# Loads from a second queue, another split of the weights' decoding over the engines, and a packed composition in the opening of a light-convolution and maxout kernel

## The chip, the core and the metric

The kernel runs on one core of one Trainium2 chip. TensorE (PE in the profile) multiplies, VectorE (DVE), ScalarE (ACT) and GpSimd (POOL) do the work on elements, and SyncE (SP) and, if the program asks for it, other engines issue transfers to and from the memory of the chip (DRAM). Work tiles lie in SBUF; the products of TensorE land in PSUM, in eight banks. The metric is the device time of one execution in microseconds (us), the median of several.

## The reference

Two steps follow one another. `x` is 8 x 4160 x 192 and `weight_gen` 8 x 4160 x 8 x 7.

```python
w = softmax(weight_gen, over the 7 taps)          # per position and head
x_unf[b, s, k] = x_pad[b, s + k]                  # 6 zero rows ahead of each batch row
out = einsum('bshk,bskhg->bshg', w, x_unf)        # 8 heads of 24 channels
x = out.reshape(33280, 192)
h = maximum(maximum(x @ w1, x @ w2), x @ w3)      # each 192 x 768
return (h @ w_out).astype(float32)                # 768 x 192
```

The four weight matrices arrive as 64-bit floats, two 32-bit words for each number. The kernel reads the words and makes 32-bit floats of them itself.

## The kernel before

Tokens are worked in 65 chunks of 512. For each chunk the seven taps are softmaxed (ACT, DVE, POOL), x is multiplied by them (`r`, seven shifted products of 192 channels, 128 x 1344 elements, mostly on POOL, for a few tiles on DVE), summed over the taps (`acc`, on DVE), and turned so that channels lie along the partitions. In the opening, the tiles of chunk 0 and 1 are turned by TensorE against the identity; tiles listed in `ADDED_AS_TURNED` skip the sum on DVE, since TensorE turns all seven products and adds them in PSUM. Of the turned chunk and of each weight a high and a low part are made (`xa_hi`, `xa_lo`, `wa_hi`, `wa_lo`; channels 128 to 191 are `xb`, `xc`, `wb_hi`, `wb_lo`), and TensorE multiplies the parts that count. The three products of an up step are reduced to their maximum by differences: TensorE forms x (w1 - w3) and the like, and DVE and ACT take maxima and add. From chunk 2 on the same program runs for each chunk (line L1287 is nearly all of it).

The opening differs. The list `OPENING` is walked by a planner (`Plan`), which places each step's instructions on the engines' queues by costs, due times and a list of shifts (`moved`). The order within each queue is then fixed; an engine waits for an instruction's inputs with everything behind it.

- Loads: `load_a` (L772, the first 128 rows of w1, w2, w3 for a pair of 128-column blocks, 128 x 512 words), `load_b` (L788, the last 64 rows, for one or two pairs, on both partition halves), `load_down` (L806, w_out, 128 x 768 words). All are issued by SP. What is loaded borrows room of other tiles, so the profile calls it `h_hi`, `raw`, `room` or `h_lo`.
- Decoding: `single` turns word pairs into 32-bit floats. ACT takes the magnitude of the high word (L832). The clamp to the 32-bit range is by POOL or DVE (L849) or by two scalings on ACT (L842). Then DVE makes three passes: shift and mask (L856), the sign out of the high word (L865), the top bits of the low word (L874). The running value `ui()` of all three lies in PSUM (`bank`). A decoded piece is called `wx` (w2 and w3), `w1a` (w1), `b` (last rows), `wo` (w_out).
- Differences: POOL subtracts w1 (`h_lo<-wx,w1a`, L1017; `b<-b`, L942). For chunk 0 these 32-bit differences are multiplied directly (`up_whole`, L1349 and L1356). ACT makes the high parts (L1042, L1089, and four half copies L1108 per pair), POOL or DVE the low ones (L1004).
- TensorE in the opening: products against the identity (`warm`, L898), turns of x (L576 for the added tiles, L613 and L614 for the others), turns of w1 (L1156, L1157), three pairs of up products, the composition w1 w_out (L1181: six products of 64 output rows for channels 128 to 191, then six of 128), the down products of chunk 0 (L1436, L1438, L1445), then chunk 1's up products, the first rows of L1287.

Of the kernel before, what the change touches and what calls it, by code (L numbers as in the profile page):

```python
# [12 lines left out]
U32 = mybir.dt.uint32  # L13
AF = mybir.ActivationFunctionType
# [185 lines left out]
def lightconv_maxout_kernel(  # L200
# [31 lines left out]
    ADDED_AS_TURNED = ((0, 1), (0, 2), (0, 3))  # L232
# [3 lines left out]
    ON_POOL_FIRST = (0, 1, 2, 3)  # L236
    TAPS_ON_VECTOR = ((0, 0), (2, 3), (3, 2))
# [7 lines left out]
    CLAMP_ON_POOL = (('a', 0, 0), ('a', 1, 0), ('a', 2, 0), ('b', 0))  # L245
    CLAMP_ON_SCALAR = (('a', 0, 1), ('a', 1, 1), ('d', 0), ('d', 1), ('d', 2))
# [5 lines left out]
         ('d',): -86.4,  # L252
         ('s', 0): -96.4,
         ('s', 1): -99.4}
# [16 lines left out]
    for c in range(supers[-1][-1] + 1, NC):  # L271
        if len(supers) == len(SUPERS) or len(supers[-1]) == SC or place[c] != place[c - 1] + 1:
# [4 lines left out]
    F_MAX = float(np.array(0x47EFFFFF, np.uint32).view(np.float32))  # L277
    F_MIN = float(np.array(0x38000000, np.uint32).view(np.float32))
# [6 lines left out]
         ('warm', 1), ('warm', 1), ('warm', 1), ('warm', 2), ('warm', 18), ('turn x', 0, 3),  # L285
         ('turn x', 0, 2), ('warm', 3), ('turn x', 0, 0), ('turn x', 0, 1), ('warm', 2),
         ('warm', 1), ('warm', 4), ('warm', 1), ('turn', 0), ('warm', 4), ('parts', 0),
         ('a', 0, 0, 1), ('a', 0, 1, 2), ('b', 0), ('up', 0, 0), ('a', 1, 0, 2), ('b', 1),
         ('up', 0, 2), ('turn', 1), ('turn', 2), ('a', 2, 0, 2), ('b', 2), ('up', 0, 4),
         ('compose', 1), ('compose', 0), ('turn x', 1, 2), ('turn x', 1, 0), ('turn x', 1, 1),  # L290
         ('turn x', 1, 3), ('down', 0), ('parts', 1), ('up', 1, 2), ('up', 1, 1), ('up', 1, 0),
         ('up', 1, 3), ('up', 1, 4), ('up', 1, 5))
# [6 lines left out]
    wb_hi = const.tile([P, NJ, NI, P], F32R, name="wb_hi")  # L299
# [28 lines left out]
        "bhi": ([P, NI, P], F32R),  # L328
# [5 lines left out]
        "bhi": 2, "raw": 1,  # L334
# [9 lines left out]
        for name, n in counts.items()  # L344
    }
    plan = Plan(counts | {"conv": 3, "flight": 8}, ((3, -26.38), (4, 3.87), (5, -21.88), (7, -1.3), (9, -9.51), (11, -9.72), (12, -18.74),
# [12 lines left out]

    def hold(name):  # L360
        return Hold(name)
# [14 lines left out]
    def act(n):  # L376
        return 0.08 + 0.00083 * n
# [17 lines left out]
    def transfer(cost, emit, deps=(), due=None, holds=(), on="SP", issue=0.46):  # L395
        held = [*holds, hold("flight")]
        begun = plan.add(on, issue, emit, deps, due, held)
        return plan.add("DMA", cost, lambda: None, [begun], due, held, end=cost + 2.4)
# [367 lines left out]

    def load_a(jp):
        for i, w in enumerate(words[:3]):
            a_in[jp, i] = transfer(
                0.67,  # L770
                lambda i=i, w=w: pin(
                    nc.sync.dma_start(  # L772
                        out=raw_a(jp)[:, i].rearrange("p n w -> p (n w)"),
                        in_=w[:P, 4 * jp * P : 4 * (jp + 1) * P],
                    )
                ),
                (), LOAD_DUE["a", jp] + 0.1 * i, [a_hold(jp)],
            )

    def load_b(first, last):  # L780
        got = []
        for i, w in enumerate(words[:3]):
            for odd, h in enumerate(halves):
                got.append(
                    transfer(
                        0.05 + 0.29 * (last - first),
                        lambda i=i, w=w, odd=odd, h=h: pin(
                            nc.sync.dma_start(  # L788
                                out=raw_b()[h, first:last, i].rearrange("p j n w -> p j (n w)"),
                                in_=w[P:].rearrange("p (j o n) -> p j o n", j=NP, o=2)[  # L790
                                    :, first:last, odd
                                ],
                            )
                        ),
                        (), LOAD_DUE["b", first], [hraw[2]], issue=0.62,
                    )
                )
        for jp in range(first, last):
            b_in[jp] = got
# [14 lines left out]
    def single(key, n, source, target, deps, holds):  # L814
# [5 lines left out]
        def like(v):  # L820
            s = source().shape
            return v if len(s) == 3 else v.rearrange("p (i n) -> p i n", n=s[2])

        u = lambda: like(buf(hu)[:, :n])
# [8 lines left out]
                    u(), high().bitcast(F32), AF.Abs, scale=2.0**111 if by_scalar else 1.0  # L833
# [4 lines left out]
        if by_scalar:  # L838
            for scale in (2.0**-111, 2.0**-112):
                a = plan.add(  # L840
                    "ACT", act(n),
                    lambda scale=scale: pin(nc.scalar.activation(u(), u(), AF.Copy, scale=scale)),  # L842
                    [a], None, [hu],
                )
            b, keep, sign = a, 0x7FFFFFF8, 0x80000000
        else:
# [5 lines left out]
            keep, sign = 0x3FFFFFF8, 0xC0000000  # L852
        c = plan.add(
# [218 lines left out]
    def differences_b(jp):  # L1072
        hq = hold("bhi")
        on, then = MODE["b", jp]
        v, d, holds, terms = difference(
            (NI, P), lambda: b32[:, jp, 1:], lambda: b32[:, jp, 0], [one_b[jp]], [], on
        )
        if jp in WHOLE_UP:
            then = "POOL" if then == "L" else then
            if on == "L":  # L1080
                of = v
                d = plan.add(
                    "ACT", act(2 * P), lambda: pin(nc.scalar.copy(b32[:, jp, 1:], of())), [d],
                    None, holds,
                )
                v, holds = (lambda: b32[:, jp, 1:]), []
        b_32[jp] = d
        e = plan.add(
            "ACT", act(2 * P), lambda: pin(nc.scalar.copy(buf(hq), v())), [d], None, [*holds, hq]  # L1089
        )  # L1090

        def low():
            b_lo[jp] = rest(
                2 * P, lambda: wb_lo[:, jp], v, lambda: buf(hq).bitcast(F32), [e],
                [hq] if then == "L" else [*holds, hq], then, terms,
                2.2 if jp in WHOLE_UP or on == "POOL" else 1.0,
            )

        if then == "L":
            later["b", jp] = [low]  # L1100
        else:
            low()
        for odd, h in enumerate(halves):
            b_hi[2 * jp + odd] = [
                plan.add(
                    "ACT", 0.42,
                    lambda to=to, h=h, odd=odd: pin(
                        nc.scalar.copy(wb_hi[to, 2 * jp + odd], buf(hq)[h].bitcast(F32))  # L1108
                    ),
                    [e], None, [hq],  # L1110
                )
                for to in halves
            ]
# [58 lines left out]

    def compose(n):
        for to, f in (((wca, slice(0, P)), (wcb, slice(P, D)))[n],):
# [136 lines left out]
    def up(c, j, i):  # L1311
# [5 lines left out]
        def terms(half):  # L1317
            got = [
# [3 lines left out]
                    (CH, lambda: wb_hi[:, j, i], lambda: buf(b), [*b_hi[j], bl], [b])  # L1322
                    if half == low
                    else (CH, lambda: wb_hi[:, j, i], lambda: buf(k), [*b_hi[j], *cs], [k])
# [52 lines left out]
    def evict(c, j, i, hb, made):  # L1377
# [7 lines left out]
        hh, hl, his, los = hs[c]  # L1385
        if i == 0:
# [39 lines left out]
    def down_whole(t):  # L1426
        assert len(of_c32) == 3
# [47 lines left out]
    def down(c, t):  # L1475
# [8 lines left out]
        assert len(of_c) == 5  # L1484
# [232 lines left out]
```

## Time and profile before

| | |
|---|---|
| median of 3 executions | 1399.69 us (1399.49 to 1399.96) |
| the profiled execution, its own time | 1399.97 us |
| its span, first to last instruction | 1398.1 us |
| TensorE busy | 1391.6 us |
| VectorE, ScalarE, GpSimd busy | 1009.5, 1128.3, 1094.8 us |
| first row of L1287 | 55.21 us after the span's start |

The execution's own time is 1.9 us more than its span. Busy shares are averages over the opening and the long run of equal chunks; the change touches the opening alone, so the views below are read there.

### The profile page before, as it was taken

The page shows a single profiled execution, that of the slowest core. Times are in us where ns is not written, and L with a number is a line of the kernel's source. Part 1 is how long each engine was busy: PE and PEld are TensorE (multiplying, and loading weights), DVE is VectorE, ACT ScalarE, POOL GpSimd, SP SyncE. Part 2 cuts the span into 40 slices and gives each one's busy share as a digit, 9 for nine tenths or more (in the row PEclk, how much of TensorE's full clock was granted, in tenths as well). Part 3 has the DMA queues.
Part 4 walks back from the last instruction along what each step waited for, and adds up shares of the span by engine and source line. Part 5 has one row for each costly group of instructions (what it writes and reads, how often), then busy time and mean ns, then how long its engine had stood idle before and what let it go on. Part 6 is the DMA issues. An engine that isn't in the chain of part 4 may idle for free.

```text
span 1398.1 us, 36944 instructions
## 1 busy us (share of the span) xinstructions
PE 1391.6 (100%) x14825; PEld 1327.1 (95%) x14825; DVE 1009.5 (72%) x1373; ACT 1128.3 (81%) x2870; POOL 1094.8 (78%) x606
## 2 busy tenths in 40 slices
PE   9999999999999999999999999999999999999998
PEld 4899999999999999999999999999999999999998
DVE  7988777677677678668668667668767768767533
ACT  6687888788888888888788888888888888789773
POOL 7999998788788788788788788788788788788321
PEclk9999999999999999999999999999999999999999
DMA  7202211011111011111011111011111111110000
GB/s 245 104 19 105 75 58 70 25 60 69 70 60 69 24 59 70 70 59 70 24 59 70 70 59 70 26 57 70 70 59 70 38 55 60 56 63 19 24 24 24
DMA packets 23532, 85.68 MB, mean 61 GB/s; under 512 B 2632, under 2 KB 9544, under 8 KB 19520
## 3 DMA queue, kind: packets, MB, share of 16 engines
q1 hardware_dynamic: 23360, 83.32, 16.2%
q8 instruction: 116, 1.90, 0.6%
q14 instruction: 56, 0.46, 0.1%
HBM read 57.75 MB, written 25.56 MB: 60 GB/s over the span
## 4 chain that ended last, share of the span: by engine, by line
PE 92%; DVE 2%; POOL 2%; ACT 1%; DMA 1%; issue 1%; SPq 0%; DVEq 0%; POOLq 0%; ACTq 0%
PE bank L1287 92%; POOL r L522 1%; DVE acc L535 1%; ACT room L688 1%; DMA h_lo<-in_moe_w_dram 0%; POOL h_lo L1417 0%; DMA h_hi<-in_moe_w_dram 0%; DVE h_hi L1397 0%; DVE bank L865 0%; DVE bank L856 0%; PE bank L1265 0%; ACT m L1389 0%; POOL xb L723 0%; POOL wt L485 0%; DVE r L522 0%
## 5 line engine op out<-in xcount | busy, mean ns | idle before, releaser
L522 POOL TENSOR_TENSOR r<-xt,wt 128x1344 f32<-128x1344 f32 x257 | 714.2, 2845 | 139.1 <-DVE acc L535 137.1
L1287 PE MATMUL bank<-wo,h_hi 64*128 64x384 f32 x3060 | 657.4, 356 | 0.0
L1287 PE MATMUL bank<-wo,h_lo 64*128 64x192 f32 x3060 | 584.5, 247 | 0.0
L688 ACT COPY room<-room 32x128 f32<-32x128 f32 x1512 | 448.6, 297 | 61.4 <-DVE room L677 38.3
L1287 PEld LDWEIGHTS bank<-wo,h_lo 64*128 64x128 f32 x3060 | 480.4, 187 | 0.0
L1287 PEld LDWEIGHTS bank<-wo,h_hi 64*128 64x128 f32 x3060 | 471.5, 185 | 0.0
L1287 PE MATMUL bank<-xa_hi,wa_hi 64*128 64x512 f32 x1536 | 459.0, 389 | 0.0
L1287 PE MATMUL bank<-xa_lo,wa_hi 64*128 64x512 f32 x1536 | 455.6, 387 | 0.0
L1287 PE MATMUL bank<-xa_hi,wa_lo 64*128 64x512 f32 x1536 | 455.1, 387 | 0.0
L535 DVE TENSOR_REDUCE acc<-r 128x192 f32<-128x1344 f32 x257 | 399.6, 1556 | 5.2 <-POOL r L522 4.3
L1287 PE MATMUL bank<-xc,wb_hi 64*128 64x512 f32 x768 | 276.8, 386 | 0.0
L1389 ACT ACTIVATE m<-bank 128x512 f32<-128x512 f32 x390 | 232.4, 597 | 54.3 <-PE bank L1287 48.5
L1287 PE MATMUL bank<-xb,wb_hi 64*128 64x512 f32 x768 | 271.6, 387 | 0.0
L1287 PE MATMUL bank<-xc,wb_lo 64*128 64x512 f32 x768 | 250.5, 386 | 0.0
L1287 PEld LDWEIGHTS bank<-xa_hi,wa_hi 64*128 64x128 f32 x1536 | 239.6, 184 | 9.1 <-issue 0.2
L1287 PEld LDWEIGHTS bank<-xa_lo,wa_hi 64*128 64x128 f32 x1536 | 239.5, 184 | 8.9
L1287 PEld LDWEIGHTS bank<-xa_hi,wa_lo 64*128 64x128 f32 x1536 | 238.9, 184 | 9.2
L1528 DVE TENSOR_TENSOR o<-bank,ob 128x192 f32<-128x192 f32 x255 | 89.0, 349 | 187.7 <-ACT ob L1521 187.5
L1417 DVE TENSOR_TENSOR h_lo<-bank,h_hi 128x512 fp32r<-128x512 f32 x254 | 174.1, 685 | 59.6 <-ACT h_hi L1410 59.1
L1417 POOL TENSOR_TENSOR h_lo<-m,h_hi 128x512 fp32r<-128x512 f32 x130 | 171.1, 1317 | 39.4 <-ACT h_hi L1410 39.2
L1406 DVE TENSOR_TENSOR bank<-bank,m 128x512 f32<-128x512 f32 x254 | 175.4, 691 | 16.2 <-ACT m L1389 10.3
L1287 PE MATMUL bank<-wca,xa_hi 64*128 64x384 f32 x510 | 179.4, 352 | 0.3 <-SPq L1293 0.3
(132 smaller groups left out, 2046.7 us busy)
## 6 DMA issues: line engine op xcount, KB each, us to landing
xt<-in_x_dram SPq DMA_DIRECT2D x30, 1344.0 KB, 5.8
out_dram<-o SPq DMA_DIRECT2D x64, 384.0 KB, 2.3
wt<-in_weight_gen_dram SPq DMA_DIRECT2D x31, 224.0 KB, 2.5
xt<-in_x_dram SPq DMA_DIRECT2D x2, 960.0 KB, 6.6
h_hi<-in_moe_w_dram SPq DMA_DIRECT2D x6, 256.0 KB, 4.6
xt<-in_x_dram SPq DMA_DIRECT2D x2, 768.0 KB, 5.0
room<-in_moe_w_out_dram SPq DMA_DIRECT2D x2, 384.0 KB, 6.9
h_lo<-in_moe_w_dram SPq DMA_DIRECT2D x6, 128.0 KB, 5.0
```

The source lines that it names most:

```text
L522: on.tensor_tensor(to, buf(hx)[:, la + t : la + t + K].rearrange("p k (h g) -> p k h g", g=G), wide() .rearrange("p (h k) -> p k h", k=K) ...
L535: pin(nc.vector.tensor_reduce(buf(ha)[:, t], of, axis=AX.X, op=ALU.add))
L688: pin(nc.scalar.copy(to[:, :, p : p + 32], b[p : p + 32, :, f : f + 32]))
L1287: ins = nc.tensor.matmul(buf(hb)[:, :n], w()[h], v()[h], start=half == 0 and first, stop=half == 1 and last,)
L1389: lambda: pin(nc.scalar.activation(buf(hm), buf(hb), AF.Relu)), [made], due,
L1406: lambda: pin(nc.vector.tensor_tensor(buf(keep), buf(hb), buf(hm), op=ALU.max)),
L1417: eng.tensor_tensor(buf(hl)[:, j], buf(keep), buf(hh)[:, j].bitcast(F32), op=ALU.subtract)
L1528: nc.vector.tensor_tensor(buf(ho)[:, t], buf(hb)[:, :D], buf(hq), op=ALU.add)
```

## The change

Seven edits, all of them ahead of the first rows of L1287.

1. The first pair of the last 64 rows (`('b', 0)`, six transfers) is issued by ACT's queue instead of SP's. In the planner, ACT's transfers have a limit of their own on how many are under way.
2. Eleven of the decoded pieces (`ENDS`) are decoded in another way. ACT takes the magnitude already scaled by 2^-112, one clamp from above follows (DVE or POOL, L942 of the new file), the low word's top bits are taken out of its upper 16 bits by ACT (L858) or POOL (L864), and are written to a tile `m` in SBUF; DVE puts the sign on them in place (L906) and joins both in one pass (L957). The three DVE passes L856, L865 and L874 and the second scaling on ACT are gone for these pieces.
3. `wb_hi` holds both halves in place: ACT writes the high part there at once (L1200), and copies each half to the other partitions (L1218): three copies for a pair where there were five. The tile `bhi` is gone.
4. The composition of channels 128 to 191 (`compose_low`) puts even blocks on output partitions 0 to 63 and odd ones on 64 to 127; two copies by ACT across the halves and one addition by DVE follow.
5. Tile 0 of chunk 1 is added as turned.
6. The opening's list is another: loads, the order of turns, the down loads' due time, where the turns of w1 stand, and which tap products DVE does (one more).
7. The shifts `moved` are other numbers.

The core of the diff:

```diff
-    ADDED_AS_TURNED = ((0, 1), (0, 2), (0, 3))
+    ADDED_AS_TURNED = ((0, 1), (0, 2), (0, 3), (1, 0))
...
-    TAPS_ON_VECTOR = ((0, 0), (2, 3), (3, 2))
+    ON_POOL_FIRST = (0, 2, 5)
+    TAPS_ON_VECTOR = ((0, 0), (1, 3), (2, 3), (3, 2))
...
-    CLAMP_ON_SCALAR = (('a', 0, 1), ('a', 1, 1), ('d', 0), ('d', 1), ('d', 2))
+    CLAMP_ON_POOL = (('a', 0, 0), ('a', 2, 0), ('b', 1), ('d', 1), ('d', 2))
+    CLAMP_ON_SCALAR = (('a', 0, 1), ('d', 0))
+    ENDS = {('a', 0, 0): ('DVE', 'ACT'),
...
+         ('a', 2, 1): ('POOL', 'ACT'),
...
+         ('b', 2): ('DVE', 'POOL'),
...
-         ('d',): -86.4,
+         ('d',): -96.9,
...
+    LOAD_ON_SCALAR = (('b', 0),)
...
+         ('b', 0), ('up', 0, 0), ('turn', 2), ('a', 1, 0, 2), ('b', 1), ('up', 0, 2), ('turn', 1),
+         ('a', 2, 0, 2), ('b', 2), ('up', 0, 4), ('compose', 1), ('turn x', 1, 0), ('compose', 0),
+         ('turn x', 1, 2), ('turn x', 1, 1), ('turn x', 1, 3), ('down', 0), ('parts', 1),
...
+                    plan.add(
+                        "DVE", vec(n),
+                        lambda: pin(
+                            nc.vector.scalar_tensor_tensor(
+                                of_x().bitcast(U32), of(), a, of_x().bitcast(U32),
+                                op0=op, op1=ALU.bitwise_or,
+                            )
+                        ),
+                        [*deps, *got], None, [hm, hc, *holds],
+                    )
...
+        if crossed:
+            x = ends_of()
+            return plan.add(
+                "DVE", vec(n),
+                lambda: pin(
+                    nc.vector.scalar_tensor_tensor(
+                        target().bitcast(U32), u().bitcast(U32), 3, of_x().bitcast(U32),
+                        op0=ALU.logical_shift_left, op1=ALU.bitwise_or,
+                    )
+                ),
...
+                        buf(hb)[halves[j % 2], :D], w1t()[:, j, P:], wo32[:, j],
+                        start=j < 2, stop=j >= NJ - 2,
```

What stands on the queues is shown at four places.

ScalarE's queue, from the program's first instruction, before:

```order
L1630 ACT_TABLE_LOAD
L1630 ACTIVATE minus<-ident 128x128
L467 ACTIVATE wt<-wt 128x224
L832 ACTIVATE m<-h_hi 128x256
L477 ACTIVATE den<-den 128x32
L504 COPY bank<-wt 128x56
```

and now (`h_lo` is the room that the last rows' words are loaded to; the exponential of the softmax is now L479):

```order
L805 DMA h_lo<-in_moe_w_dram 64x256 x6
L1803 ACT_TABLE_LOAD
L1803 ACTIVATE minus<-ident 128x128
L479 ACTIVATE wt<-wt 128x224
L489 ACTIVATE den<-den 128x32
L516 COPY bank<-wt 128x56
```

Six issues now stand ahead of the table load and the exponential.

VectorE's queue, from its first tap product to the first decoded w1 piece; before:

```order
L535 TENSOR_REDUCE acc<-r 128x192
L856 TENSOR_SCALAR bank<-bank 128x384
L865 SCALAR_TENSOR_TENSOR bank<-room,bank 128x384
L856 TENSOR_SCALAR bank<-bank 128x512
L874 SCALAR_TENSOR_TENSOR wo_69<-room,bank 128x384
L865 SCALAR_TENSOR_TENSOR bank<-h_hi,bank 128x512
L874 SCALAR_TENSOR_TENSOR wx<-h_hi,bank 128x512
L856 TENSOR_SCALAR bank<-m 128x256
```

and now (`m` and `h_lo`, `h_hi` are tiles in SBUF, `bank` is in PSUM):

```order
L906 SCALAR_TENSOR_TENSOR m<-h_hi,m 128x256
L547 TENSOR_REDUCE acc<-r 128x192
L942 TENSOR_SCALAR bank<-bank 128x384
L906 SCALAR_TENSOR_TENSOR m<-h_lo,m 128x384
L942 TENSOR_SCALAR bank<-bank 128x512
L957 SCALAR_TENSOR_TENSOR b_68<-bank,m 128x384
L906 SCALAR_TENSOR_TENSOR m<-h_hi,m 128x512
L957 SCALAR_TENSOR_TENSOR wx<-bank,m 128x512
L957 SCALAR_TENSOR_TENSOR w1a<-m 128x256
L906 SCALAR_TENSOR_TENSOR m<-h_lo,m 128x384 x2
L957 SCALAR_TENSOR_TENSOR b_68<-m 128x384
```

An L865 reads one tile in SBUF and the bank; an L906 reads two tiles in SBUF, and so does an L957 whose clamped value is in `m`.

VectorE's queue about the last w_out pieces, which the composition reads (`wo_69`), with the maxima of chunk 0's last up step (`h_hi<-bank,m`), now:

```order
L906 SCALAR_TENSOR_TENSOR m<-h_lo,m 128x384
L547 TENSOR_REDUCE acc<-r 128x192
L484 TENSOR_REDUCE den<-wt 128x64
L942 TENSOR_SCALAR bank<-bank 128x384
L957 SCALAR_TENSOR_TENSOR wo_69<-m 128x384
L493 RECIPROCAL den<-den 128x64
L1570 TENSOR_TENSOR h_hi<-bank,m 128x512
L906 SCALAR_TENSOR_TENSOR m<-room,m 128x384
L1570 TENSOR_TENSOR h_hi<-bank,m 128x512
L957 SCALAR_TENSOR_TENSOR wo_69<-bank,m 128x384
```

where before it was

```order
L1397 TENSOR_TENSOR h_hi<-bank,m 128x512
L865 SCALAR_TENSOR_TENSOR bank<-h_lo,bank 128x384
L1397 TENSOR_TENSOR h_hi<-bank,m 128x512
L874 SCALAR_TENSOR_TENSOR wo_69<-h_lo,bank 128x384
L481 RECIPROCAL den<-den 128x64
```

These maxima are those of the last up step but one, in both programs. Between L906 and L957 of the last piece stands one maximum, as before between L865 and L874; the reduction `acc<-r`, two small ones and another piece's decoding are ahead of it.

TensorE's queue from the last up products of chunk 0 to the down products, before:

```order
L1181 MATMUL bank<-wo_69,raw 64x192 x6
L1181 MATMUL bank<-wo_69,raw 128x192 x6
L613 MATMUL bank<-ident,acc 128x128
L614 MATMUL bank<-ident,acc 64x128
L613 MATMUL bank<-ident,acc 128x128
```

and now:

```order
L1290 MATMUL bank<-wo_69,raw 64x192 x6
L588 MATMUL bank<-ident,r 128x128 x7
L588 MATMUL bank<-ident,r 64x128 x7
L1338 MATMUL bank<-wo_69,raw 128x192 x6
L625 MATMUL bank<-ident,acc 128x128
L626 MATMUL bank<-ident,acc 64x128
```

Fourteen turns have come between the two parts of the composition, for one pair of turns (L613, L614) that is gone behind it.

## Rows read from the trace of the kernel before

**Rows 1.** Waits of TensorE: engine, line <- releaser, us in total, times, longest
```profile
PE bank L1349 <- POOL h_lo L1017: 0.8, 1, 0.8
PE bank L898 <- ACT xa_hi L637: 0.5, 1, 0.5
```

**Rows 2.** Timeline of TensorE, opening: start, duration, line, form, count [idle before, releaser]
```profile
11.57 3.22 PE L576 MATMUL bank<-ident,r 128*128 128x128 f32 x28
...
17.14 1.68 PE L898 MATMUL bank<-ident 128*128 128x256 f32 x6
...
20.83 1.88 PE L1349 MATMUL bank<-xa_hi,h_lo 128*128 128x512 f32 x4
...
27.77 1.98 PE L1349 MATMUL bank<-xa_hi,h_lo 128*128 128x512 f32 x4 [0.82 <-POOL h_lo L1017]
...
40.27 4.31 PE L1181 MATMUL bank<-wo,raw 128*64 128x192 f32 x24
44.42 0.27 PE L613 MATMUL bank<-ident,acc 128*128 128x128 f32 x1
...
44.64 0.27 PE L613 MATMUL bank<-ident,acc 128*128 128x128 f32 x1
...
55.21 0.49 PE L1287 MATMUL bank<-xa_hi,wa_hi 64*128 64x512 f32 x1
```

**Rows 3.** Busy time by stretch: us; PE, PEld, DVE, ACT, POOL; PEclk, DMA share, GB/s
```profile
10.00:20.00 10.00, 9.50 (x64) 7.30 (x63) 9.30 (x16) 7.71 (x16) 8.92 (x9) 1.00 0.96 235
20.00:28.00 8.00, 7.18 (x21) 2.35 (x20) 6.79 (x16) 6.89 (x18) 6.01 (x9) 1.00 1.03 400
28.00:36.00 8.00, 8.00 (x26) 3.01 (x25) 8.00 (x15) 7.91 (x20) 7.92 (x6) 1.00 0.14 50
36.00:45.00 9.00, 9.00 (x43) 5.46 (x43) 9.00 (x11) 4.62 (x15) 8.79 (x6) 1.00 0.28 97
```

**Rows 4.** Timeline of VectorE, 49.8 to 56 us
```profile
50.36 0.82 DVE L1004 TENSOR_TENSOR wa_lo<-h_lo,wa_hi 128x512 fp32r<-128x512 f32 x1
...
52.56 0.67 DVE L718 TENSOR_TENSOR xa_lo<-bank,xa_hi 128x512 fp32r<-128x512 f32 x1
...
54.29 0.82 DVE L1004 TENSOR_TENSOR wb_lo<-b,bhi 128x256 fp32r<-128x256 f32 x1
```

**Rows 5.** Timeline of GpSimd, 49.8 to 56 us
```profile
49.90 2.41 POOL L1004 TENSOR_TENSOR wa_lo<-h_lo,wa_hi 128x256 fp32r<-128x256 f32 x2
52.27 2.66 POOL L522 TENSOR_TENSOR r<-xt,wt 128x1344 f32<-128x1344 f32 x1
```

**Rows 6.** Instructions of L1004 and L865: shortest, median, longest ns; first and last start
```profile
L1004 POOL TENSOR_TENSOR wa_lo<-h_lo,wa_hi x3: 721/735/1724, 25.8 to 50.6; 128x256 fp32r<-128x256 f32 x2, 128x512 fp32r<-128x512 f32 x1
...
L865 DVE SCALAR_TENSOR_TENSOR bank<-h_lo,bank x4: 553/554/556, 17.2 to 35.7; 128x384 uint32<-128x384 uint32 x4
```

**Rows 7.** Timeline of VectorE, 0 to 45 us
```profile
7.83 1.55 DVE L522 TENSOR_TENSOR r<-xt,bank 128x1344 f32<-128x1344 f32 x1 [1.04 <-DMA xt<-in_x_dram]
...
16.90 0.42 DVE L865 SCALAR_TENSOR_TENSOR bank<-h_hi,bank 128x256 uint32<-128x256 uint32 x1
...
36.74 0.55 DVE L874 SCALAR_TENSOR_TENSOR wo<-h_lo,bank 128x384 uint32<-128x384 uint32 x1
```

**Rows 8.** Timeline of GpSimd, 5 to 32 us
```profile
7.89 7.60 POOL L522 TENSOR_TENSOR r<-xt,wt 128x1344 f32<-128x1344 f32 x3 [1.81 <-DMA xt<-in_x_dram]
...
26.44 1.27 POOL L1017 TENSOR_TENSOR h_lo<-wx,w1a 128x512 f32<-128x512 f32 x1
```

**Rows 9.** Timelines of ScalarE's start
```profile
0.73 1.28 ACT L1630 ACT_TABLE_LOAD   x1 [0.73 <-PEq L1697]
...
3.85 0.39 ACT L467 ACTIVATE wt<-wt 128x224 f32<-128x224 f32 x1 [1.52 <-POOL wt L463]
```

**Rows 10.** Timeline of SyncE's issues
```profile
4.02 0.83 SPq L788 DMA_DIRECT2D h_lo<-in_moe_w_dram  x1
...
11.95 0.47 SPq L788 DMA_DIRECT2D h_lo<-in_moe_w_dram  x1
```

More of the change, by code (lines that the diff above doesn't have):

```diff
@@ L395, in transfer @@
     def transfer(cost, emit, deps=(), due=None, holds=(), on="SP", issue=0.46):
-        held = [*holds, hold("flight")]
+        held = [*holds, hold("flight" if on == "SP" else "along")]
         begun = plan.add(on, issue, emit, deps, due, held)
-        return plan.add("DMA", cost, lambda: None, [begun], due, held, end=cost + 2.4)
+        return plan.add("DMA", cost, lambda: None, [begun], due, held, end=cost + 2.75)
     loads = {}
@@ new lines, in of_words @@
+        def of_words(on, of, to, a, b, one, two, deps):
+            scaled = lambda: to(), lambda: source().bitcast(U16)[..., of]
+            if on == "ACT":
+                return plan.add(
+                    "ACT", act_near(n),
+                    lambda: pin(nc.scalar.activation(to(), scaled[1](), AF.Copy, scale=a, bias=b)),
+                    deps, None, [hm, hc, *holds],
+                )
+            return plan.add(
+                "POOL", 0.16 + 0.00093 * n,
+                lambda: pin(
+                    nc.gpsimd.tensor_scalar(to(), scaled[1](), a, b, op0=one, op1=two)
+                ),
+                deps, None, [hm, hc, *holds],
+            )
@@ L1072, in differences_b @@
     def differences_b(jp):
-        hq = hold("bhi")
+        own = lambda: wb_hi[:, jp, 0]
         on, then = MODE["b", jp]
@@ L1103, in differences_b @@
         for odd, h in enumerate(halves):
[L1104 to L1113, printed above, removed]
+            copied = plan.add(
+                "ACT", 0.42,
+                lambda to=halves[1 - odd], h=h: pin(
+                    nc.scalar.copy(wb_hi[to, jp, 1], own()[h].bitcast(F32))
+                ),
+                [e], None, [],
+            )
+            b_hi[2 * jp + odd] = [(e, copied)[other] for other in ((0, 1) if odd == 0 else (1, 0))]
     o_hi, o_lo, o_32 = {}, {}, {}
@@ L1170, in turn_weights, with compose_low, mult @@
             turned_w[j] = out
+    def compose_low():
+        hb, ht = hold("bank"), hold("m")
+        deps = [turned_w[j] for j in range(NJ)] + [o_32[j] for j in range(NJ)]
+        below, above = halves
+        def mult():
+            for j in range(NJ):
+                pin(
+                    nc.tensor.matmul(
+                        buf(hb)[halves[j % 2], :D], w1t()[:, j, P:], wo32[:, j],
+                        start=j < 2, stop=j >= NJ - 2,
+                    )
+                )
+        got = whole(1.15, mult, deps, [hb, hw1t])
+        crossed = [
+            plan.add(
+                "ACT", act(D),
+                lambda to=to, of=of: pin(nc.scalar.copy(buf(ht)[to, :D], buf(hb)[of, :D])), [got],
+                clock[0] + 0.5, [hb, ht],
+            )
+            for to, of in ((above, below), (below, above))
+        ]
+        both = plan.add(
+            "DVE", vec(D),
+            lambda: pin(
+                nc.vector.tensor_tensor(buf(hwc)[:, 1, :D], buf(hb)[:, :D], buf(ht)[:, :D], op=ALU.add)
+            ),
+            crossed, clock[0] + 0.7, [hb, ht, hwc],
+        )
+        of_c32.append(both)
+        hi = plan.add(
+            "ACT", act(D), lambda: pin(nc.scalar.copy(wcb[:, :D], buf(hwc)[:, 1, :D])), [both],
+            clock[0] + 1.5, [hwc],
+        )
+        lo = plan.add(
+            "DVE", vec(D),
+            lambda: pin(
+                nc.vector.tensor_tensor(
+                    wcb[:, D:], buf(hwc)[:, 1, :D], wcb[:, :D].bitcast(F32), op=ALU.subtract
+                )
+            ),
+            [hi], clock[0] + 2, [hwc],
+        )
+        of_c.extend((hi, lo))
     def compose(n):
+        if n == 1 and WHOLE_DOWN:
+            return compose_low()
         for to, f in (((wca, slice(0, P)), (wcb, slice(P, D)))[n],):
@@ L1317, in terms @@
         def terms(half):
+            w_b = lambda: wb_hi[:, jp, int(half != odd), i]
             got = [
@@ L1385, in evict @@
         hh, hl, his, los = hs[c]
+        if whole_h and TOGETHER:
+            hs[c, j, i] = hb, made
+            if i == 1:
+                h0, made0 = hs[c, j, 0]
+                his[j] = plan.add(
+                    "DVE", vec(CH) + TOGETHER,
+                    lambda: pin(
+                        nc.vector.scalar_tensor_tensor(
+                            buf(hh, None, F32)[:, j], buf(hb), 0.0, buf(h0), op0=ALU.max,
+                            op1=ALU.max,
+                        )
+                    ),
+                    [made, made0], due, [hb, h0, hh],
+                )
+            return
         if i == 0:
```

124 lines of the change are left out of this document (96 added, 28 removed), and 23 rows, old and new, of the table plan.

## The prediction

> **What bounds the kernel now.** I read TensorE's waits first: over the whole span two stand beside the one for the identity at the start, 0.8 us for a difference by GpSimd (L1017) and 0.5 us for `xa_hi` [rows 1]. From the first row of L1287, at 55.21 us of the span [rows 2], it waits for nothing worth a row, so the rest is set by its own work. The change edits what lies ahead of that row. The question is therefore one number: when the first chunk-1 product starts. Every microsecond there moves the end by one, as long as nothing behind it starts to wait. The sums are made against the profiled execution's 1399.97 us (1398.1 us of span and 1.9 us around it), 0.28 us above the median of 1399.69 us; results are then put against the median.
>
> Next, TensorE's timeline up to 55 us [rows 2]: added turns from 11.57, the first up product at 20.83, the third pair of up products after a wait of 0.82 at 27.77, the composition at 40.27 for 4.31 us, then turns and down products. Last, the busy time by stretch [rows 3]: between 20 and 45 us VectorE is busy for 23.79 of 25 us and GpSimd for 22.72. Both feed TensorE there, so TensorE is the bound with two engines close behind it. What such an engine loses comes out on TensorE as soon as the cover is used up.
>
> **The change part by part.** *TensorE's own work.* The extra added tile costs 14 turns in place of one pair. Turns of that form took 3.22 us for 28, 0.115 each, so 1.61 us; a pair takes 0.22 (44.42 to 44.64): **+1.39** [rows 2]. The 64-row half of the composition is 12 of the 24 records of L1181, 2.1 us by their mean. If even and odd blocks, on separate output halves, run beside each other, half of that goes: 24 records in the 4.15 us from 40.27 to 44.42, six saved, **-1.04**; if one after the other, 0 [rows 2]. The turns of w1 are moved, not added. Work against the identity ahead of the first product grows from 49 to 51 blocks of 128 columns (from the list); a late stretch of seven took 1.68, so +0.48, and the 0.5 wait for `xa_hi`, which stands in that stretch, goes: **about 0** [rows 1, 2]. Bounds of the start by TensorE alone: -0.5 to +0.5.
>
> *The wait at 27.77.* A decoded piece now takes two VectorE passes or three with its clamp, where it took three or four. If GpSimd's difference comes in time, **-0.82** [rows 2]. Lower bound -0.82; upper bound 0 by itself.
>
> *ScalarE's queue.* Six issues stand ahead of the table load of 1.28 us, which started at 0.73; the exponential came at 3.85, after it had waited 1.52 for GpSimd [rows 9]. An issue of this form took 0.47 on SP, or 0.83 when a landing was waited for in it [rows 10]. So the table load ends at 0.73 + 2.8 + 1.28 = 4.8, some 1.0 to 1.3 us behind the old start of the exponential. The cover: GpSimd's first tap products waited 1.81 us for x, VectorE's 1.04 [rows 7, 8]. **0**; with 0.83 each the table load ends at 7.0 and about 1.4 us of the 3.2 are left beyond the cover. In exchange the rows of the first up pair are asked for earlier, and the other weights' loads come behind x; what each load then does on its queue the order doesn't tell. I take 0 for the loads, bounds -0.5 and +1.
>
> *The decoding on VectorE.* By counts of the queues from the first tap product to the last w_out piece and durations of this trace, VectorE's work is the same within half a microsecond: fewer shift-and-mask passes, but one more tap product of 1.55 and longer strided sums. Before, the last piece was done at 37.29 (36.74 and 0.55 [rows 7]), 2.98 us ahead of the composition [rows 2]. With the wait of 0.82 gone the composition is wanted earlier, which leaves 2.2 at most; VectorE's start on later landings takes from that too. I keep **0.6 us of cover**, bounds 0 and 2.2.
>
> But the new passes read other places. L865 read one tile in SBUF and one in PSUM. Between 17.2 and 35.7 us its four 384-element instances took 553 to 556 ns although GpSimd was busy nearly all the time [rows 3, 6]: no contention. All ten new L906 read two tiles in SBUF, and so do four L957 and one low part (L1115) ahead of the composition: 15 instructions. The trace has two VectorE instructions of that kind, both L1004: 0.82 us for 512 elements, where a 512-element one with a PSUM input took 0.67, and 0.82 for 256, where 0.42 is usual [rows 4, 7]. Both began while GpSimd ran. The first GpSimd product beside them ended about 50.6 (the pair of 2.41 us from 49.90, less the longer one's 1.72), the second at 54.93 (52.27 + 2.66) [rows 5, 6]; each VectorE instruction ended 0.2 to 0.6 us after that. And the GpSimd L1004 that met the first one took 1.72 where a GpSimd difference of 512 elements takes 1.27 [rows 6, 8]. They read as instructions that held each other up.
>
> The Trainium skill, "SBUF — State Buffer", section "SBUF: two separate sides", states that VectorE with two SBUF inputs and GpSimd share a port pair as an exclusive lock: whoever starts first has it for the whole instruction and the other blocks fully. These rows agree with it; by that rule each of the 15 waits for whatever GpSimd is in.
>
> The price: 0.15 and 0.40 in the two instances, 0.27 in the mean; 15 times that is **+4.1** on VectorE. From above: beside one of the tap products, which take 2.53 each (7.60 for three [rows 8]), a wait is up to 2.5 and half of it in the mean. Three to five of the 15 stand where GpSimd's queue has tap products, so 3.8 to 6.3 for these alone, and some 0.3 for each of the other ten: 7 to 9 in all. From below: 0, if the new operation doesn't behave as L1004. I take 4.1, since many of the ten will find GpSimd waiting for their own result. GpSimd loses as well (0.45 on that L1004); the differences L1128 ahead of an up product each stand on the path: **+0.3**, bounds 0 and 1.5.
>
> Where it comes out: the first up product, which waits for two small differences; the second up pair; and above all the composition, which needs the last w_out piece. That piece's L906 stands in a stretch of tap products on GpSimd. VectorE is full there, so delays of the earlier instructions add up until the composition.
>
> *The copies of `wb_hi`* free ScalarE of some 0.4 us for each of two copies a pair; it has time left (4.62 busy of 9 us from 36 to 45 [rows 3]) and no wait of TensorE names it there: 0.
>
> Sum: +1.39 - 1.04 + 0 - 0.82 = **-0.5** for TensorE's own; VectorE +4.1 less the cover of 0.6, GpSimd +0.3: **+3.8**. First chunk-1 product at 55.21 + 3.3 = 58.5; 1399.69 + 3.3 = **1403.0 us**.
>
> **The rivals.**
> *A. Not slower: no hold.* The new passes run beside GpSimd at their usual 0.42 to 0.69. For it: the two L1004 are another operation, and GpSimd's spans are rough. Against it: L865 is the same operation as L906, with one operand moved, and the two L1004 overlap as told. Only the sum for TensorE is left: 1399.69 - 0.5 = 1399.2, with bounds 1397.7 (all covers and the loads in favour) and 1400.7. It decides from where the mean hold of the 15 is under 0.24 us: 15 x 0.24 = 3.6, and with -0.5, -0.6 and +0.3 that is 2.8 us, the bound of what can be told.
>
> *B. Holds of the upper kind.* L906 meets whole tap products as often as the queues allow: 7 in place of 4.1, +2.9: 1405.9. For it: GpSimd is busy 22.72 of 25 us. Against: order and data ties between both engines.
> The Trainium skill, "Vector Engine (DVE) Microarchitecture Reference", section "Points that are easy to get wrong", says that this operation with two SBUF sources that aren't bf16 runs at half throughput. No row of this case shows that operation with two such sources; by it the ten L906 and four L957 would take about double, near B or above.
>
> *C. The column halves don't run beside each other*: +1.04 on the forecast, 1404.0. The trace has no such pair of products, so it stays open.
>
> *D. Late start*: ScalarE's issues take 0.83 each, or x and the first weights land later; +1.4: with the holds 1404.4, without 1400.6.
>
> **How the numbers follow.** Forecast 0.52 (1401.5 to 1404.0), A 0.18, B 0.12, C 0.08, D 0.10. The likeliest is 1403.0 us. Eight in ten: the forecast, C, D, and of A and B the near parts, 1399.0 to 1405.7; forecast's own range 1401.5 to 1404.0. About 0.2%, 2.8 us, is what a measurement can tell from no change here: slower begins at 1402.5, faster below 1396.9. Slower: somewhat over six tenths of the forecast's 0.52, B, most of C and half of D, 0.32 + 0.12 + 0.06 + 0.05 = 0.55. Faster: 0.03; the first chunk-1 product would have to start at 52.4, which no term of the sum gives. Same: 0.42.
>
> **What would show it.** Right: L906 with the same size at spread durations (0.55 to 2 us for 384), ending shortly after a GpSimd instruction; TensorE waiting for a w_out piece (L957) ahead of the composition and for GpSimd or VectorE ahead of the second up pair; the six products of the 64-column tiles in 1.0 to 1.1 us; L1444 starting at about 58.5. Wrong: L906 at even durations beside busy GpSimd (A); TensorE's largest new wait naming a load or ScalarE (D); the time after the first chunk-1 product differing by more than 0.5 us from the 1342.9 us it takes before, which would mean that the change reaches further than the opening.

## The result, and the profile after

The changed kernel takes 1407.47 us (median of 5, 1406.83 to 1407.80), the kernel before in the same runs 1399.96 us. The ratio is 1.0052, 95% interval 1.0038 to 1.0066: slower by 7.5 us, where 3.3 was forecast. The profiled execution has a span of 1405.5 us against 1398.1.

TensorE's waits of the changed kernel over the whole span (line <- releaser, us in total, times, longest), which answer to [rows 1]:

```profile
PE bank L1507 <- POOL h_lo L1128: 4.4, 2, 2.7
PE bank L1009 <- POOL ident masks.py:199: 1.3, 1, 1.3
PE bank L1444 <- SPq L1450: 1.0, 1, 1.0
PE bank L1444 <- POOL xa_lo L730: 0.8, 1, 0.8
PE bank L625 <- DVE acc L547: 0.7, 1, 0.7
PE bank L1290 <- DVE wo L957: 0.6, 1, 0.6
```

In the kernel before, one wait stands behind the first chunk-1 product:

```profile
PE bank L1287 <- SPq L1293: 0.3, 1, 0.3
```

TensorE's timeline of the changed kernel, the same places as [rows 2]:

```profile
22.17 1.98 PE L1507 MATMUL bank<-xa_hi,h_lo 128*128 128x512 f32 x4 [1.69 <-POOL h_lo L1128]
...
31.44 2.50 PE L1507 MATMUL bank<-xa_hi,h_lo 128*128 128x512 f32 x4 [2.74 <-POOL h_lo L1128]
33.88 2.08 PE L1514 MATMUL bank<-xc,b 64*128 64x512 f32 x4
...
39.37 1.88 PE L1507 MATMUL bank<-xa_hi,h_lo 128*128 128x512 f32 x4
...
45.87 1.20 PE L1290 MATMUL bank<-wo,raw 128*64 128x192 f32 x12 [0.59 <-DVE wo L957]
47.00 1.75 PE L588 MATMUL bank<-ident,r 128*128 128x128 f32 x14
48.58 2.12 PE L1338 MATMUL bank<-wo,raw 128*128 128x192 f32 x12
...
61.13 0.50 PE L1444 MATMUL bank<-xa_hi,wa_hi 64*128 64x512 f32 x1
```

The first chunk-1 product starts at 61.13 instead of 55.21: 5.92 of the 7.4 us of span. By stretches against the kernel before: the first up product 1.34 later; the second pair of up products another 2.33; the third 1.28 (39.37 for 34.42), since the second pair ran 1.6 longer, less 0.32 for a turn of w1 that stands ahead of it now; the composition 0.65, behind a wait of 0.59 for the last w_out piece; from there to the down products, with the turns, 0.30; the down products 0.02. The other 1.48 us lie behind the first chunk-1 product (1344.37 us from there to the end, 1342.89 before): a wait of 0.8 for a low part of the next chunk (L730) and one of 1.0 at SP. The kernel before waits there for 0.3 only. The prediction had named this as a sign of being wrong: more than 0.5 us of difference behind the first chunk-1 product means that the change reaches further than the opening. It does: the new list also puts the six up steps of chunk 1 in another order (5, 3, 4, 2, 0, 1 for 2, 1, 0, 3, 4, 5), so not all of the edits lie ahead of the first rows of L1287.

The second pair ran long for the clock. Busy time from 33 to 36 us, the granted clock being the number behind the five engines:

```profile
33.00:36.00 3.00, 3.00 (x7) 0.62 (x5) 2.02 (x3) 2.93 (x8) 3.00 (x2) 0.50 0.01 3
```

TensorE ran at 1.2 GHz there, after it had stood for 2.74 us (up to 31.44); before the stand and again from 36.5 us on it had 2.4 GHz.

VectorE's timeline, at the places of the new passes:

```profile
14.11 2.53 DVE L906 SCALAR_TENSOR_TENSOR m<-h_lo,m 128x384 uint32<-128x384 uint32 x1
...
17.63 0.67 DVE L906 SCALAR_TENSOR_TENSOR m<-h_hi,m 128x512 uint32<-128x512 uint32 x1
...
24.31 1.27 DVE L906 SCALAR_TENSOR_TENSOR m<-h_hi,m 128x512 uint32<-128x512 uint32 x1
...
28.15 0.84 DVE L1115 TENSOR_TENSOR wb_lo<-b,wb_hi 128x256 fp32r<-128x256 f32 x1
...
40.13 1.70 DVE L957 SCALAR_TENSOR_TENSOR wo<-m 128x384 uint32<-128x384 uint32 x1
...
42.76 1.91 DVE L906 SCALAR_TENSOR_TENSOR m<-room,m 128x384 uint32<-128x384 uint32 x1
...
45.19 0.54 DVE L957 SCALAR_TENSOR_TENSOR wo<-bank,m 128x384 uint32<-128x384 uint32 x1
```

and GpSimd's beside them:

```profile
8.25 7.97 POOL L534 TENSOR_TENSOR r<-xt,wt 128x1344 f32<-128x1344 f32 x3
16.19 1.16 POOL L942 TENSOR_SCALAR m<-m 128x256 f32<-128x256 f32 x1
17.79 1.10 POOL L1053 TENSOR_TENSOR b<-b 128x256 f32<-128x256 f32 x1 [0.44 <-DVE b L957]
...
24.31 0.72 POOL L1053 TENSOR_TENSOR b<-b 128x256 f32<-128x256 f32 x1
...
28.04 2.13 POOL L864 TENSOR_SCALAR m<-raw 128x512 uint16<-128x512 uint16 x1
...
38.85 5.49 POOL L534 TENSOR_TENSOR r<-xt,wt 128x1344 f32<-128x1344 f32 x2
44.21 1.28 POOL L497 TENSOR_TENSOR wt<-wt,den 128x448 f32<-128x448 f32 x1
```

One size stands here at two lengths. The 512-element L906 takes 0.67 us at 17.63, begun while GpSimd stands (from 17.35 to 17.79), and 1.27 at 24.31, where GpSimd works: it ends at 25.58, 0.55 behind the end of GpSimd's L1053 (24.31 + 0.72 = 25.03). The 384-element one at 14.11 takes 2.53, and ends at 16.6, after the third tap product (8.25 + 7.97 = 16.22). An L957 with one input in PSUM takes 0.54 at 45.19 although GpSimd works (L497 up to 45.49, and L1115 behind it). Over the 15 instructions with two inputs in SBUF, what they take beyond 0.42, 0.55 and 0.68 us for 256, 384 and 512 elements comes to 7.1 us; the three that stood longest beside tap products (14.11, 40.13, 42.76) make 4.5 of it.

Not every such instruction waits for the end of GpSimd's. L1115 at 28.15 takes 0.84, which is 0.42 too long, but ends at 28.99, while GpSimd's L864 runs from 28.04 to 30.17 and takes its usual 2.1 us.

### The profile page after: what moved, and what is told of

It is laid out like the page before. It is cut to its first block, busy times and chain, and to the rows that moved or that the text cites. A ratio compares the mean times of both kernels' runs of the same rounds, so it can differ in the third digit from the quotient of the medians.

```text
span 1405.5 us, 36959 instructions
## 1 busy us (share of the span) xinstructions
PE 1393.0 (99%) x14835; PEld 1365.6 (97%) x14835; DVE 1014.4 (72%) x1367; ACT 1125.4 (80%) x2864; POOL 1099.5 (78%) x607
## 4 chain that ended last, share of the span: by engine, by line
PE 94%; DVE 2%; ACT 1%; POOL 1%; DMA 1%; issue 0%; SPq 0%; ACTq 0%; POOLq 0%; DVEq 0%
PE bank L1444 94%; DVE acc L547 1%; ACT room L700 0%; DMA h_lo<-in_moe_w_dram 0%; DVE m L906 0%; DMA h_hi<-in_moe_w_dram 0%; SPq L451 0%; POOL m L942 0%; POOL h_lo L1128 0%; ACT m L1562 0%; POOL m L864 0%; DVE h_hi L1570 0%; ACT m L858 0%; PE bank L1422 0%; DVE r L534 0%
## 5 line engine op out<-in xcount | busy, mean ns | idle before, releaser
L1444 PE MATMUL bank<-wo,h_lo 64*128 64x192 f32 x3060 | 593.9, 247 | 0.0
L1444 PEld LDWEIGHTS bank<-wo,h_lo 64*128 64x128 f32 x3060 | 486.6, 187 | 0.0
L1444 PEld LDWEIGHTS bank<-wo,h_hi 64*128 64x128 f32 x3060 | 486.4, 185 | 0.0
L1444 PE MATMUL bank<-xa_hi,wa_hi 64*128 64x512 f32 x1536 | 466.2, 389 | 0.0
L1444 PE MATMUL bank<-xa_lo,wa_hi 64*128 64x512 f32 x1536 | 464.1, 387 | 0.8 <-POOL xa_lo L730 0.8
L1444 PE MATMUL bank<-xa_hi,wa_lo 64*128 64x512 f32 x1536 | 464.4, 387 | 0.0
L1444 PE MATMUL bank<-xb,wb_hi 64*128 64x512 f32 x768 | 278.0, 387 | 0.0
L1444 PEld LDWEIGHTS bank<-xa_lo,wa_hi 64*128 64x128 f32 x1536 | 249.3, 184 | 2.5 <-POOL xa_lo L730 1.2
L1444 PEld LDWEIGHTS bank<-xa_hi,wa_lo 64*128 64x128 f32 x1536 | 249.9, 184 | 0.9
L1444 PEld LDWEIGHTS bank<-xa_hi,wa_hi 64*128 64x128 f32 x1536 | 249.2, 184 | 1.1 <-issue 0.2
```

The source lines that it names most:

```text
L1444: ins = nc.tensor.matmul(buf(hb)[:, :n], w()[h], v()[h], start=half == 0 and first, stop=half == 1 and last,)
```

## The experiments

**x in PSUM.** In the changed kernel, nine of the eleven pieces that are decoded in the new way (`crossed` in the code) get their low bits in a PSUM bank; the edit leaves out the two that GpSimd helps with, so the ten of the expectation are one too many. Queues and instructions stay in order, and 13 of the 15 VectorE instructions have one input in SBUF now.

```diff
+        apart = crossed and "POOL" not in (sign_on, low_on)
+        hx = (hb if by_pool else Hold("bank")) if apart else hm
+        x_in = lambda: like(buf(hx)[:, :n])
+        x_out = x_in if by_pool else of_x
...
-                                of_x().bitcast(U32), of(), a, of_x().bitcast(U32),
+                                x_out().bitcast(U32), of(), a, x_in().bitcast(U32),
...
```

> The changed kernel with one thing moved: for ten of the eleven crossed pieces the low word's bits are written to a PSUM bank instead of the SBUF tile m, and the sign pass puts its result in PSUM too where the clamped value lies in SBUF. Every engine's queue keeps its order; 13 of the 15 VectorE instructions with two SBUF inputs ahead of the composition have one now. Theory 1 (VectorE and GpSimd hold each other up on two SBUF inputs): nearly all of the 7.5 us goes back, 1399.0 to 1401.5 us; the 384-element sign passes take 0.55 us each, the wait ahead of the second up pair is under 0.8 us, TensorE's clock stays whole. Rival (the late start of ScalarE and later landings set the opening): no more than 1 us goes back, 1406.5 us or more.

1401.86 us (11 executions) against 1399.93: ratio 1.0014, interval 1.0005 to 1.0023. Of the 7.5 us, 5.6 are back. VectorE's timeline:

```profile
14.05 0.55 DVE L910 SCALAR_TENSOR_TENSOR m<-h_lo,bank 128x384 uint32<-128x384 uint32 x1
...
37.22 0.54 DVE L961 SCALAR_TENSOR_TENSOR wo<-m,bank 128x384 uint32<-128x384 uint32 x1
...
38.73 0.54 DVE L910 SCALAR_TENSOR_TENSOR m<-room,bank 128x384 uint32<-128x384 uint32 x1
```

The three that took 2.53, 1.70 and 1.91 take 0.55 now. TensorE starts its first up product at 20.82, the composition at 40.99 and chunk 1 at 56.25, 4.88 us earlier than in the changed kernel, with a mean granted clock of 1.0. The time is 0.4 us above what theory 1 allowed, and the second up pair still waits 1.50 where it allowed 0.8: something else stands there.

**The kernel before, with the running value in SBUF.** Nothing but the place of `ui()` differs from the kernel before.

```diff
+        "ui": ([P, CH], F32),
...
-        ui = lambda: like(buf(hb)[:, :n]).bitcast(U32)
+        hi = Hold("ui")
+        ui = lambda: like(buf(hi)[:, :n]).bitcast(U32)
```

> The kernel before, its decoding unchanged, but the running value of the three VectorE passes lies in an SBUF tile of its own instead of the PSUM bank; orders of all queues stay. 24 VectorE passes read two SBUF tiles then. Theory 1: slower by 6 to 14 us (24 instructions at 0.3 to 0.6 us of holding each), 1406 to 1414 us, with passes of 384 elements spread from 0.55 to over 2 us. Rival (two SBUF inputs cost nothing): 1399.7 us within 1 us.

1409.82 us against 1399.93: ratio 1.0070, interval 1.0054 to 1.0085, slower by 9.9 us. The sign pass by tile in the whole program (count: shortest, median, longest ns):

```profile
L867 DVE SCALAR_TENSOR_TENSOR ui<-h_hi,ui x4: 677/680/1210, 6.9 to 22.7; 128x256 uint32<-128x256 uint32 x2, 128x512 uint32<-128x512 uint32 x2
L867 DVE SCALAR_TENSOR_TENSOR ui<-h_lo,ui x4: 542/545/557, 20.5 to 45.5; 128x384 uint32<-128x384 uint32 x4
L867 DVE SCALAR_TENSOR_TENSOR ui<-room,ui x2: 2605/2716/2826, 13.3 to 38.8; 128x384 uint32<-128x384 uint32 x2
L867 DVE SCALAR_TENSOR_TENSOR ui<-raw,ui x2: 425/1736/3047, 25.5 to 31.9; 128x256 uint32<-128x256 uint32 x1, 128x512 uint32<-128x512 uint32 x1
```

The same instruction with 384 elements takes 0.54 or 2.83 us, where with one input in PSUM all took 0.55 to 0.56 [rows 6]. So the place of the second input by itself, over 24 instructions here, costs at least as much as the whole change with its 15.

**Loads back on SP.** The changed kernel, its six ScalarE loads issued by SP.

```diff
-        return (nc.scalar, "ACT") if key in LOAD_ON_SCALAR else (nc.sync, "SP")
+        return (nc.sync, "ACT") if key in LOAD_ON_SCALAR else (nc.sync, "SP")
```

> The changed kernel with the first pair's six row loads issued by SP again, interleaved with SP's other loads in the planner's order; all else as in the changed kernel. Theory 1: ScalarE's first exponential comes about 3 us earlier, VectorE's first work too, but the 128-row loads are issued later by six issues; the first up product moves by no more than 1 us either way, and the second up pair waits as before: 1406 to 1409 us. Rival (ScalarE's late start is what costs): 3 us or more go back, 1404.5 us or less.

1406.80 us against 1399.93: ratio 1.0050, interval 1.0036 to 1.0063. The second up pair waits 2.74 us as before. The rival that ScalarE's late start sets the opening falls; by the medians 0.7 us go back.

**TensorE kept busy in its wait.** Three products against the identity ahead of the turn of w1.

```diff
+            if jp == 2:
+                full = buf(Hold("bank"))
+                for _ in range(3):
+                    pin(
+                        nc.tensor.matmul(
+                            full.rearrange("p (k n) -> p k n", k=4), ident,
+                            ident.unsqueeze(1).broadcast_to([P, 4, P]), start=True, stop=True,
+                        )
+                    )
```

> The changed kernel with three more products of 512 columns against the identity (2.6 us) on TensorE between the first up pair and the turn of w1 ahead of the second, where TensorE waited 2.74 us. Theory 1 with the clock as a part of it (granted clock 0.50 from 33 to 36 us after that wait, 1.5 us longer up products): the clock stays whole, the second up pair starts where it did, and 1 to 1.6 us go back: 1405.9 to 1406.5 us. Rival (the longer up products are held by their operands and not by the clock): no change or up to 0.5 us slower, 1407 to 1408 us.

1408.06 us against 1399.93: ratio 1.0063, interval 1.0049 to 1.0077; no gain over the changed kernel, where 1 to 1.6 us had been forecast. TensorE's timeline:

```profile
31.40 1.98 PE L1516 MATMUL bank<-xa_hi,h_lo 128*128 128x512 f32 x4
33.31 1.13 PE L1523 MATMUL bank<-xc,b 64*128 64x512 f32 x4
...
45.82 2.19 PE L1299 MATMUL bank<-wo,raw 128*64 128x192 f32 x12 [2.18 <-DVE wo L957]
47.94 2.35 PE L588 MATMUL bank<-ident,r 128*128 128x128 f32 x14
```

The clock part of the theory held: the second pair starts at the same time (31.40 for 31.44) and runs at full length, since the clock stayed at 2.4 GHz. But the composition starts where it did, at 45.82 for 45.87, with a wait of 2.18 instead of 0.59, and the clock fell behind that wait instead. So neither TensorE nor its clock set the composition's time: VectorE's queue did, which ends the last w_out piece at the same place in both (45.67 and 45.73). That queue is not full by its own work alone: at 36.01 it had stood 0.99 us for ScalarE's L858.

**Two operations in GpSimd's clamp.** The run with x in PSUM, and

```diff
-                lambda: pin(eng.tensor_scalar(u(), u(), MOST, None, op0=ALU.min)),
+                lambda: pin(
+                    eng.tensor_scalar(u(), u(), MOST, 0.0, op0=ALU.min, op1=ALU.max)
+                    if by_pool else eng.tensor_scalar(u(), u(), MOST, None, op0=ALU.min)
+                ),
```

> The run with x in PSUM, and GpSimd's clamp of the crossed pieces written with two operations (minimum, then maximum with 0) instead of one. In the run with x in PSUM that one-operation clamp took 0.84 and 0.85 us for 256 elements and 1.17 and 1.54 for 384, where the two-operation clamps took 0.40 (before) and 0.51. Theory 2 (the form with one operation is itself slower on GpSimd): 0.40 and 0.51 us now, some 1.9 us less on GpSimd ahead of the second up pair, TensorE's wait of 1.5 us there shrinks to 0.6 or less, 1400.4 to 1401.3 us. Rival (they are long because of what runs beside them): durations and time stay, 1401.9 us within 0.4.

1400.83 us against 1399.85: ratio 1.0007, interval 0.9998 to 1.0016. GpSimd's timeline of the run with x in PSUM alone:

```profile
16.28 0.85 POOL L946 TENSOR_SCALAR m<-m 128x256 f32<-128x256 f32 x1
...
34.76 1.17 POOL L946 TENSOR_SCALAR m<-m 128x384 f32<-128x384 f32 x1
```

and with two operations:

```profile
15.90 0.40 POOL L947 TENSOR_SCALAR m<-m 128x256 f32<-128x256 f32 x1
...
34.15 0.51 POOL L947 TENSOR_SCALAR m<-m 128x384 f32<-128x384 f32 x1
```

Theory 2 holds: the clamp with one operation takes over twice as long as with two. The wait of the second up pair went from 1.50 to 0.77, not to the 0.6 that was expected, the first chunk-1 product from 56.25 to 55.64, and by the medians about 1.0 us of the time is back; the intervals of the two runs overlap, so that size is less sure than the durations.

**Whole words for the sign.** The run before this one, with GpSimd's sign pass on `raw` writing 32-bit words.

```diff
-                        "POOL", 3, lambda: half(1), 2.0**15, 2.0**15, ALU.is_ge, ALU.mult, deps
+                        "POOL", 3, lambda: of_x().bitcast(U32), 2.0**15, 2.0**31, ALU.is_ge, ALU.mult, deps
```

> The run before this one, and GpSimd's sign pass on the 512-element piece writes whole 32-bit words instead of every other 16-bit half. It took 2.11 us in the run with x in PSUM, where the pass that writes whole words took 0.53 for 384 elements. Theory 2: about 0.7 us, the second up pair waits for nothing, 1400.0 to 1400.8 us; what is left over the kernel before lies in the wait for the low part of chunk 1 or 2 and for SP behind the first chunk-1 product (0.9 and 1.1 us). Rival (16-bit input makes it slow): 2.1 us still, no further gain.

1400.98 us against 1399.85, ratio 1.0007 (0.9998 to 1.0016): no gain. The pass takes 2.02 us for 512 elements instead of 2.12. So it isn't the half words that are written. Nor is it 16-bit input alone, which the rival named: the pass that takes 0.53 us for 384 elements also reads 16-bit words. It differs in its operations (multiply and add, not compare and multiply) and in the tile it reads; no run tries these apart, so which of them counts stays open.

**The columns alone.** The kernel before with the composition's 64-row half on two output halves. With it come the two copies by ScalarE and the one addition by VectorE that join the halves, in place of copies that are gone; the orders are as before.

```diff
+                    if n == 1:
+                        pin(
+                            nc.tensor.matmul(
+                                buf(hb)[halves[j % 2], :D], w1t()[:, j, f], wo32[:, j],
+                                start=j < 2, stop=j >= NJ - 2,
+                            )
+                        )
+                        continue
...
+                for to, of in (halves[::-1], halves):
+                    pin(nc.scalar.copy(buf(ht)[to], buf(hb)[of, :D]))
+                pin(
+                    nc.vector.tensor_tensor(
+                        buf(hwc)[:, 1, :D], buf(hb)[:, :D], buf(ht), op=ALU.add
+                    )
+                )
...
```

> The kernel before with one part of the change alone: the composition's 64-row half on two output halves, in the same place, its results made by the same queues in the same order. If the two halves run beside each other, as in the changed kernel's profile (12 records in 1.2 us), the first chunk-1 product starts 1.0 us earlier (54.2 us), 1398.6 to 1399.2 us. Rival (what TensorE saves there it waits for behind it, in VectorE's added step): no change.

1401.22 us against 1399.85: ratio 1.0011, interval 1.0002 to 1.0020, if anything slower. TensorE's timeline:

```profile
20.04 1.88 PE L1370 MATMUL bank<-xa_hi,h_lo 128*128 128x512 f32 x4
...
38.99 1.20 PE L1182 MATMUL bank<-wo,raw 128*64 128x192 f32 x12
...
42.17 0.27 PE L613 MATMUL bank<-ident,acc 128*128 128x128 f32 x1
...
44.06 0.33 PE L613 MATMUL bank<-ident,acc 128*128 128x128 f32 x1 [1.07 <-DVE acc L535]
...
54.25 0.50 PE L1308 MATMUL bank<-xa_hi,wa_hi 64*128 64x512 f32 x1
...
56.10 0.50 PE L1308 MATMUL bank<-xb,wb_hi 64*128 64x512 f32 x1 [1.12 <-DVE xb L723]
```

The halves run beside each other (1.20 us for 12 records), and the composition takes 3.18 us (38.99 to 42.17) instead of 4.15, so 0.97 less. But this execution was early before that, on the same instructions as the kernel before: the first up product starts at 20.04 for 20.83, the composition at 38.99 for 40.27. TensorE is 2.25 us ahead at the composition's end. It then waits 1.07 us for a sum by VectorE (`acc`), and the first chunk-1 product starts 0.96 us earlier, at 54.25; that this is just what the columns save is chance. Then TensorE waits 1.12 us for `xb` by VectorE, and all is given back. VectorE's queue ends `xb` at 56.04 there (55.37 and 0.67 us). In the kernel before, VectorE and TensorE show for it:

```profile
55.03 0.67 DVE L723 TENSOR_TENSOR xb<-bank,xc 64x512 fp32r<-64x512 f32 x1
```

```profile
55.78 0.47 PE L1287 MATMUL bank<-xb,wb_hi 64*128 64x512 f32 x1
```

It ended at 55.70, 0.08 us ahead of its use: VectorE was as much a bound there as TensorE. No version tried here beats the kernel before.

## Why the prediction was wrong

The direction and the main mechanism, the holds, were right, the size was not: 7.5 us against 3.3, and 1407.47 lies above the range's upper end of 1405.7. What the runs say of its steps:

- **What bounds the kernel.** That every microsecond of the first chunk-1 product moves the end by one was too strong both ways. 1.5 us came on top behind it in the changed kernel. And in the run with the columns alone an earlier start by 0.96 us was worth nothing. "Two engines close behind it" was the right reading of [rows 3], but the sum treated TensorE's own savings as if they counted.
- **TensorE's own work.** +1.39 for the extra tile: 14 turns took 1.58 us (47.00 to 48.58), less 0.22: +1.36. -1.04 for the columns: 24 records, 1.13 and 1.95 us, for 4.15: -1.07. Rival C falls. These two held to a tenth. The start by TensorE alone, 0: with x in PSUM the first up product starts at 20.82 (20.83 before), but executions differ by more than that (21.05 with two operations in the clamp, 20.01 with whole words, 20.04 with the columns alone), so it is shown to within 0.8 us. The list has 50 blocks against the identity there, not 51.
- **The wait at 27.77**, -0.82: wrong in sign. It became 2.74 us, and 1.50 with x in PSUM. GpSimd was late, not VectorE alone: its clamps with one operation take 0.85 and 1.17 us by themselves where I had priced none anew, and its sign pass takes 2.1 us. No row of the kernel before shows either form.
- **ScalarE's queue and the loads**, 0 with bounds: the six issues took 3.78 us and the table load ended at 5.80, between the 4.8 and the 7.0 of the working; with the loads on SP 0.7 us goes back by the medians. Rival D falls as the main cause.
- **The holds, "15 times that is +4.1 on VectorE"**: this is the step that failed. They came to 7.1 us, 0.47 each and not 0.27. The two instances in the kernel before had begun late in a GpSimd instruction. In the changed kernel three met most of a tap product (2.0, 1.2 and 1.4 us beyond their own length), as the upper bound of 7 to 9 had it, and no cover was left, as the wait of 0.59 ahead of the composition and the run with TensorE kept busy show. With 7.1 in place of 4.1 the sum gives 6.3 us on the first chunk-1 product, where 5.92 was measured; that it comes so close is luck in part, since the -0.82 in that sum did not come. The 1.48 us behind it had no term. My reason for the lower value, that many would find GpSimd waiting for them, held for four of the 15 only, which took their own length.
- **GpSimd "+0.3"**: L1053 took 1.10 instead of 0.73 and the pair of small differences 1.73 instead of 1.46, 0.64 together, twice what was taken, and the clamps, held for up to 0.4 us each on top of their slow form, were not in it.
- **Rival A** (no hold) falls by two runs, one that takes the second SBUF input away (-5.6 us) and one that adds it to the kernel before (+9.9). **Rival B** is nearest in size, by holds of the upper kind.

Rival B's other way, a halved rate, is not what happened. The Trainium skill, "Vector Engine (DVE) Microarchitecture Reference", section "Points that are easy to get wrong", says that this operation with two SBUF sources that aren't bf16 runs at half throughput. The trace disagrees: 512 elements took 0.67 us when begun while GpSimd stood, as with one source in PSUM (0.68 in the run with x in PSUM). The Trainium skill, "SBUF — State Buffer", section "SBUF: two separate sides", has an exclusive lock held for the whole instruction. The rows beside tap products and differences agree with it (14.11 and 24.31); L1115 at 28.15 does not, since it ended 1.18 us before the GpSimd instruction that had begun ahead of it; the run with x in PSUM has the same pair again (0.84 us beside 2.11).

The clock, which the prediction left out, cost 1.6 us on the second up pair (7.55 us from 31.44 to 38.99, 5.94 in the run with TensorE kept busy), but that run shows that VectorE's queue hid it. Of the 7.5 us, 5.6 go with the 13 holds that were taken away and what came of them, 1.0 with the clamps. The last 0.98 is in part the start (55.64 for 55.21) and in part the wait at SP behind it (0.9 for 0.3), which all versions with the new order have. The run with whole words points to the second: its first chunk-1 product starts at 54.99, ahead of the kernel before, and it still takes 1400.98 us, with waits of 1.0 at SP and 0.6 for `xa_lo` behind that product. What of these comes from the new order of chunk 1's up steps and what from the shifts in `moved` was not tried apart.

## What to carry to other kernels

Before a value of VectorE is moved from PSUM to SBUF, count the instructions that then read two SBUF tiles, and price each by what GpSimd runs at that place of the order, not by a mean of the few instances at hand. Where two engines are full, a saving on a third one is worth nothing until their queues have room; look for the slack of each at the place where the stretch ends. A shorter form of an instruction is not a cheaper one until a row shows it.

## What the runs showed of the hardware

- GpSimd's `tensor_scalar` in fp32 with one operation took 0.85 us for 256 and 1.17 for 384 elements, with two operations 0.40 and 0.51.
- GpSimd's compare-and-multiply pass on 16-bit words took 2.0 to 2.1 us for 512 elements, its multiply-and-add pass on such words 0.53 for 384.
- VectorE instructions of 384 elements with two inputs in SBUF took 0.74 to 2.53 us beside GpSimd's work in the changed kernel, and with one of them in PSUM 0.54 to 0.56 us. Beside GpSimd's L864 of 2.13 us one was held for 0.42 us only.
- TensorE's granted clock fell to 1.2 GHz after a wait of 2.74 us, and in the run with TensorE kept busy after one of 2.18, where the next 12 records took 2.19 us instead of 1.20. Ahead of both waits it had 2.4 GHz. In the kernel before with the running value in SBUF it stayed at 2.4 GHz after a wait of 2.51 us (up to 21.53).
